# Value rows of the global tokens gathered early and copied in by small transfers, and key and query loads of 80 rows, in an attention kernel with dense layers behind it

## The chip, the cores and the metric

The kernel runs on one core of one Trainium2 chip. The metric is the device time of one execution in microseconds. An execution of the profiled kind gives in addition a trace: every instruction of the engines TensorE (PE, with its weight loads as PEld), VectorE (DVE), ScalarE (ACT), GpSimd (POOL) and SyncE (SP), with the semaphores between them and the packets of the DMA queues.

## The reference

Attention over a window of 32 tokens to either side, with eight global tokens that attend to all and are attended by all, and then a dense layer with an activation of x cos(x) and a second dense layer.

```python
B, H, S, D = 8, 8, 576, 64                     # 8 global tokens in global_idx
scores = matmul(q, k^T) / sqrt(D)
mask   = |i - j| <= 32  or  i is global  or  j is global
attn   = softmax(where(mask, scores, -1e9))
x      = (attn @ v) as (B * S, H * D) = (4608, 512)
h      = x @ w_in                              # (512, 2048)
out    = (h * cos(h)) @ w_out                  # (2048, 512), float32
```

## The kernel before

**Units.** Two heads of one batch are a pair; there are 32 pairs. Two pairs, so four heads, are a half batch. The first five half batches (pairs 0 to 9) are the front; they are computed while weights and most inputs are still on their way, and they take another route than the rest. The front cuts the 576 tokens of a head into five blocks of 120 keys (`NK5`), to each of which the eight global keys are added as the first eight rows (`G`). So the value tile of a half batch, `vw`, has 128 partitions: eight rows of global values, 120 rows of local ones.

**The order** of all work is written by hand. The string `FRONT` lists the steps of the front, one word each; `MID`, `FIFTH`, `SIXTH` and `ORDER` list the later half batches. A step issues its instructions on each engine's queue at the place where it stands, and each engine runs its own queue in order. The letters that matter here, with the number of the pair or half batch behind them:

- `L`: `load_qk`, two DMAs from GpSimd's queue that bring key and query of a half batch into `kn` and `qn`, as fp16, eight tokens in one row of 1 KB per head, so 72 rows for 576 tokens (three buffers; the third, `kn[2]` and `qn[2]`, lies in the space of `w_out16`).
- `M`: `next_values`, which clears 64 rows of the first block of a value buffer on VectorE, and then `load_vn`, five DMAs from SP that bring the half batch's values into `vn32` as fp32. `vn32` has room for four half batches, and half batch 4 takes the place of half batch 2.
- `C`: `cast_vn`, one GpSimd instruction that turns these into fp16 in `vw`. Ahead of it, from half batch 2 on, stands a copy of one element that waits for the newest mask product.
- `y`: `value_rows`, for the two heads of a pair: five matmuls with `one_v`, a matrix of zeros and ones that picks the global tokens out of the blocks, add up to the eight rows of global values in a bank of PSUM (tag `h`), and a copy on ScalarE writes them to the first eight rows of all five blocks of `vw`. Since `one_v` multiplies every row, the first eight rows of `vn32` have to hold numbers; `clear_rows` sets them to zero.
- `k`, `q`: transposes of key and query on TensorE into a bank of tag `h`, and copies on ScalarE to `kw` and `qb`. For pairs 4 to 9 the global columns are put in by GpSimd (`g`), from `kgT` and `qgT`, which step `H1` turns on TensorE and copies on VectorE.
- `s`: scores of a pair, ten matmuls into four banks, then four exponentials on ScalarE (`e`) and three products with the mask on VectorE (`pm`).
- `f`: matmuls of ones, whose result nobody reads, into a spare part of `pv`.
- `p`: values of a pair, 20 matmuls into the one buffer `pv`, then sums, reciprocals and the product `xn` on VectorE.
- `x`: transposes of `xn` on TensorE, copies into `xT` on VectorE.
- `E`, `Y`, `H`: gathers of the global rows of key and query, and (`Y0`) of value, for the first four batches by GpSimd, each as two indirect DMAs with the row numbers `gidx_rows`; `H2` turns the gathered values to fp16 for later half batches.
- `n`: sum of squares of `xn` on ScalarE. `W`, `O`: weight loads. `m`, `t`: the first dense matmuls and their activation.

The dense layers' instructions are `mlp_in` (`ph`), `mlp_act` (`cos`, `g`) and `mlp_out` (`po`); they start behind pair 8 and then run among the later pairs.

**Semaphores of the DMAs.** The DMAs of SP use eight semaphores in turn, and those of GpSimd eight others. A DMA whose semaphore has been used waits on its queue until the one eight before it has landed. A DMA that reads or writes what others make waits for those in addition.

Of the kernel before, what the change touches and what calls it, by code (L numbers as in the profile page):

```python
# [10 lines left out]
FP16 = mybir.dt.float16  # L11
# [6 lines left out]
B, H, S, D = 8, 8, 576, 64  # L18
# [5 lines left out]
G = 8  # L24
# [2 lines left out]
KL = 32  # L27
HY = 5
PK = 4
RW = 8  # L30
KS = 120
NK5 = 5
KPAD = 3
KP = KPAD + S // RW
QP = S // RW + 4
OFF = (0, 136, 488, 680, 328)
# [5 lines left out]
C = G + QB  # L42
# [10 lines left out]

SIXTH = "sa 2 2 2 2 sz pa 1 1 2 xa pz G 1 1 2 xz n 1 1 D0 2 kc qc D1 1 D2 2 1"

FRONT = ("M1 s0 E0 C0 E1 L2 w6 k1 q1 w4 s1 y0.0 f8 k2 q2 C1 H0 p0 M2 L3 y0.1 s2 k3 q3 f6 x0 p1 M3 H1 g4 g5 g6 C2 y1.0 s3 g7 L4 I k4 q4 f6 x1 p2 M4 y1.1 s4 "
         "C3 W0 k5 q5 f6 x2 p3 y2.0 s5 g8 g9 W1 W2 W3 k6 q6 f6 x3 p4 y2.1 s6 C4 Y0 k7 q7 f6 x4 p5 n0 y3.0 s7 k8 q8 f6 x5 p6 y3.1 s8 H2 k9 q9 f6 x6 p7 y4.0 s9 "
         "x7 p8 y4.1 O m m x8 K5 p9 t t + m m t t x9 -")
WARM = 13
OK_ALL = float(P * (B * NP * 2 * BP + B))  # L60

# [143 lines left out]
def kernel(  # L205
# [10 lines left out]
    nc = tc.nc  # L216
# [5 lines left out]
    keep = es.enter_context(tc.tile_pool(name="keep", bufs=1))  # L222
# [27 lines left out]
    NN = 3  # L250
    kT = [keep.tile([P, 2, KT], FP16, name=f"kT{i}") for i in range(2)]
    qT = [keep.tile([P, 2, QT], FP16, name=f"qT{i}") for i in range(2)]
    kn = [keep.tile([KP, 2 * 2, RW, D], FP16, name=f"kn{i}") for i in range(2)]
    qn = [keep.tile([QP, 2 * 2, RW, D], FP16, name=f"qn{i}") for i in range(2)]
    w_out16 = const.tile([P, NF, DM], FP16)
    kn.append(w_out16[0:KP, 0:4].rearrange("p h (r d) -> p h r d", d=D))
    qn.append(w_out16[0:QP, 4:8].rearrange("p h (r d) -> p h r d", d=D))
# [17 lines left out]
    def load_qk(s, hs=(0, 4)):  # L275

        base = (s * 4 + hs[0]) * S * D
        for src, dst in ((k, kn[s % NN][KPAD : KPAD + S // RW]), (q, qn[s % NN][0 : S // RW])):
            nc.gpsimd.dma_start(dst[:, hs[0] : hs[1]].rearrange("x h r d -> x h (r d)"),
                                dview(src, base, (RW * D, S // RW), (S * D, hs[1] - hs[0]), (1, RW * D)))  # L280

    def turn_half(s):

# [6 lines left out]
    vg32 = keep.tile([P, 2, 2, D], FP32)  # L290
# [16 lines left out]
    def pick_globals(pr, t, src, ones, n, to):  # L307

        h0 = 2 * (pr % 2)
        for r in range(RW):  # L310
            for h in range(2):
                nc.tensor.matmul(t[h * D : (h + 1) * D], src[:n, h0 + h, r], ones[:n, r], start=r == 0, stop=r == RW - 1, skip_group_check=True)
        nc.scalar.copy(to, view(t, (0, to.shape[1]), (1, G)))

    def warm(n, tag="s"):

        t = ps.tile([P, 4, P], FP32, tag=tag, bufs=2 + (tag == "s"))
        for _ in range(n):
# [13 lines left out]
    def gather(src, dst, half):  # L332
        rows = src.rearrange("b h s d -> (b h s) d")
        for h in range(2):
            nc.gpsimd.indirect_dma_start(
                out=dst[:, half, h], out_offset=None, in_=rows,
                in_offset=bass.IndirectOffsetOnAxis(ap=gidx_rows[:, 0:1], axis=0),
                element_offset=(half * 32 + h) * S * D)
# [23 lines left out]
    def vn_of(s):  # L362
        i = s if s < 4 else 2
        return view(vn32[i // 2][:, 4 * (i % 2)], (4 * D, NK5), (1, 4 * D))
# [13 lines left out]
        nc.vector.memset(vn_of(s)[0:64, 0], 0.0)  # L378
        load_vn(s)

    def clear_rows(s):

        nc.gpsimd.memset(vn_of(s)[0:G, 1:], 0.0)

    gate = keep.tile([1, 1], FP16)

# [513 lines left out]
    with tc.manual_schedule():  # L900
# [2 lines left out]
        nc.vector.memset(ones16, 1.0)  # L903
        nc.vector.memset(pio2, pi / 2.0)
        nc.vector.memset(kn[0][0:KPAD, 0:2], 0.0)
        for t in (qn[0][64:QP, 2:4], kn[0][0:KPAD, 2:4], qn[1][64:QP], kn[1][0:KPAD], qn[2][64:QP], kn[2][0:KPAD]):
            nc.scalar.memzero(t.rearrange("p a b c -> p (a b c)"))
        load_qk(0, (0, 2))
        nc.gpsimd.iota(p_i, pattern=[[0, 1]], base=0, channel_multiplier=1)
# [12 lines left out]
        build_band()  # L922
        index_rows(1)
        load_vn(0)
        for s in range(1, 4):
            clear_rows(s)
        load_qk(1)
        build_ones()
        build_mask5()
# [60 lines left out]
            load_values(2 * s)  # L990
            load_values(2 * s + 1)

        def late_gathers(_):

            gather(v, vg32, 0)

        LOCAL = {"k": local_k, "q": local_q}
        OTHER = LOCAL | {"g": globals_kq, "L": load_qk, "W": load_w_in, "v": load_values, "n": x_squares,
                 "C": cast_vn, "I": row_numbers, "E": early_rows, "w": lambda n: warm(n, "h" if n == 6 else "s"), "y": value_rows, "M": next_values, "N": clear_rows, "Y": late_gathers, "V": hold, "U": hold_x, "H": early_globals, "Z": steady_buffers, "f": fill, "r": load_vn, "A": later_rows, "D": later_globals, "O": load_w_out, "K": lambda s: cast_half(s, "vkq"), "B": bring, "m": lambda _: one(False), "t": lambda _: mlp_act()}
        ready[0] = 1  # L1000
        for step in FRONT.split():
            if step in "+-":
                spare[0] = step == "+"
                continue
            f = (STEPS | OTHER)[step[0]]
            f(*[int(x) for x in (step[1:] or "0").split(".")])
        ready[0], front[0] = 2, False
        for s in range(4, B * NP // 2):
            outs_by[0] = 8 * (s - 3)
            for step in {4: MID, 5: FIFTH, 6: SIXTH}.get(s, ORDER).split():  # L1010
# [20 lines left out]
                else:  # L1031
                    f, pr = (STEPS | OTHER)[step[0]], 2 * s + "azcd".index(step[1])
# [56 lines left out]
```

## Time and profile before

| | us |
|---|---|
| median of 3 runs | 351.18 |
| lowest and highest | 351.07 and 353.2 |
| the profiled execution | 349.19 |
| its span, first to last instruction | 347.3 |
| PE, DVE, ACT, POOL busy in the span | 329.4, 249.5, 246.0, 110.0 |

Times in the profile count from the start of the span. A row of the timeline has start, duration, engine, line, operation, out<-in, shape, how many, and in brackets the idle time of the engine ahead of it and what ended that. A row of the chain of waits has start, duration and what the end of the kernel hung on in that time; "issue" is time in which the profile shows no wait. A row of a stretch has its bounds, its length, the busy time of PE, PEld, DVE, ACT and POOL with the number of instructions, the granted clock of TensorE, the mean busy share of the DMA engines (over 1 where packets overlap) and GB/s.

### The profile page before, as it was taken

The numbers are of one execution on the slowest core, as the hardware profiler recorded it, in microseconds if no ns is written. First come the engines' busy times: TensorE is split into PE (matmuls) and PEld (weight loads), VectorE is DVE, ScalarE is ACT, GpSimd is POOL, SyncE is SP. The second block draws the span as 40 slices with busy tenths as digits, with TensorE's granted clock in tenths as the row PEclk, the third lists the DMA queues.
The fourth block names the chain that finished last, engine by engine and source line by source line (L and its number), as shares of the span: only waits on it lengthen the run. The fifth ranks groups of instructions, "written<-read, shape, count | busy, mean of one in ns | idle before, by whom it ended". The sixth has DMA issues, their size and how long they took to land.

```text
span 347.3 us, 8464 instructions
## 1 busy us (share of the span) xinstructions
PE 329.4 (95%) x3207; PEld 172.7 (50%) x3207; DVE 249.5 (72%) x611; ACT 246.0 (71%) x423; POOL 110.0 (32%) x221
## 2 busy tenths in 40 slices
PE   7977989999989999999999999999999999999993
PEld 3566865444445454545454545454545344444442
DVE  6665778987597688888797878788888466556310
ACT  8878797796566896878787777878787866644300
POOL 8754846632352506050705062325001000000000
PEclk9999899999999999999999999999999999999997
DMA  5998992999999999999999999999990001100112
GB/s 78 185 165 152 171 195 39 187 175 153 162 153 195 149 155 137 183 150 194 140 171 156 192 142 182 126 219 145 139 134 2 32 30 59 34 31 30 62 60 69
DMA packets 165891, 44.58 MB, mean 128 GB/s; under 512 B 153764, under 2 KB 160996, under 8 KB 165668
## 3 DMA queue, kind: packets, MB, share of 16 engines
q1 hardware_dynamic: 105860, 26.70, 51.5%
q0 software_dynamic: 59984, 17.28, 49.6%
q8 instruction: 27, 0.44, 0.5%
q14 instruction: 20, 0.16, 0.2%
HBM read 44.41 MB, written 19.17 MB: 183 GB/s over the span
## 4 chain that ended last, share of the span: by engine, by line
PE 81%; ACT 6%; DVE 4%; issue 3%; DMA 2%; SPq 1%; POOL 1%; ACTq 0%; POOLq 0%; DVEq 0%
PE po L800 34%; PE ph L762 34%; PE pv L719 3%; PE st L699 3%; PE tx L744 2%; DMA gidx_col<-in_global_idx_dram 1%; ACT e L638 1%; DMA vn<-in_v_dram 1%; PE po L782 1%; PE t L319 1%; PE pv L646 1%; ACT e L634 1%; ACT cos L768 1%; DVE g L769 1%; DVE xn L666 1%
## 5 line engine op out<-in xcount | busy, mean ns | idle before, releaser
L762 PE MATMUL ph<-xT,w_in 128*128 128x512 f16 x576 | 139.3, 379 | 1.1 <-DVE g L769 1.0
L800 PE MATMUL po<-w_out,g 128*128 128x512 f16 x560 | 136.8, 379 | 0.0
L768 ACT ACTIVATE cos<-ph,pio 128x512 f16<-128x512 f32 x144 | 97.0, 687 | 55.3 <-PE ph L762 51.6
L769 DVE TENSOR_TENSOR g<-cos,ph 128x512 f16<-128x512 f16 x144 | 96.5, 685 | 45.6 <-ACT cos L768 43.4
L800 PEld LDWEIGHTS <-g 128*128 128x128 f16 x560 | 53.6, 98 | 63.7
L762 PEld LDWEIGHTS <-w_in 128*128 128x128 f16 x576 | 53.9, 98 | 62.7 <-issue 1.4
L702 ACT ACTIVATE e<-st 128x512 f16<-128x512 f32 x44 | 23.9, 594 | 10.0 <-PE st L699 9.9
L980 POOL COPY gate<-xn 1x1 f16<-1x1 f16 x8 | 1.4, 180 | 81.9 <-DVE xn L730 81.9
L703 DVE TENSOR_TENSOR pm<-e,mask 128x512 f16<-128x512 f16 x44 | 18.7, 425 | 11.7 <-ACT e L702 10.3
L752 POOL COPY xT<-xg 128x4 f16 x48 | 15.4, 320 | 31.5 <-DVE xT L747 28.9
L272 POOL DMA_DIRECT2D q<-in_q_dram x11 | 24.0, 2183 | 0.0
L818 ACT ACTIVATE xn<-xn 128x1536 f16<-128x1536 f16 (+1 forms) x16 | 22.6, 1413 | 0.0
L730 DVE TENSOR_TENSOR xn<-pv,r_all 128x768 f16<-128x768 f32 x22 | 21.1, 957 | 1.0
L805 ACT COPY o<-po 128x512 f32<-128x512 f32 x17 | 10.0, 586 | 14.7 <-PE po L800 14.7
L807 DVE COPY o<-po 128x512 f32<-128x512 f32 x18 | 12.4, 690 | 9.0 <-PE po L800 8.5
L272 POOL DMA_DIRECT2D k<-in_k_dram x11 | 18.1, 1644 | 0.9 <-issue 0.9
L768 ACT ACT_TABLE_LOAD x12 | 15.4, 1283 | 0.2
L702 ACT ACT_TABLE_LOAD x11 | 14.1, 1283 | 0.2
L607 DVE COPY kw<-kT 128x1320 f16<-128x1320 f16 x22 | 13.9, 630 | 0.0
L699 PEld LDWEIGHTS <-kw 64*128 64x128 f16 x484 | 8.4, 95 | 10.7 <-issue 8.1
L579 POOL COPY kw<-kgT 128x88 f16<-128x88 f16 x22 | 12.8, 716 | 0.1
L699 PE MATMUL st<-qb,kw 64*128 64x64 f16 x484 | 11.2, 191 | 1.5 <-DVE qb L619 1.1
(185 smaller groups left out, 391.0 us busy)
## 6 DMA issues: line engine op xcount, KB each, us to landing
out_dram<-o SPq DMA_DIRECT2D x35, 256.0 KB
vw<-v SPq DMA_DIRECT2D x32, 165.0 KB
v<-in_v_dram POOLq DMA_DIRECT2D x11, 288.0 KB, 5.5
k<-in_k_dram POOLq DMA_DIRECT2D x11, 288.0 KB, 8.7
q<-in_q_dram POOLq DMA_DIRECT2D x11, 288.0 KB, 11.5
vn<-in_v_dram SPq DMA_DIRECT2D x20, 120.0 KB
w_in<-in_moe_w_in_dram POOLq DMA_DIRECT2D x4, 512.0 KB, 10.0
w_out<-in_moe_w_out_dram POOLq DMA_DIRECT2D x1, 2048.0 KB, 15.3
```

The costliest lines, as they stand in the source:

```text
L272: nc.gpsimd.dma_start(dst[s].rearrange("t (h d) -> t h d", h=4), dview(src, base, (D, S), (S * D, 4), (1, D)))
L607: nc.vector.tensor_copy(to, view(kT[pr // 2 % 2][:, pr % 2], (QB, NB), (1, W)))
L699: nc.tensor.matmul(st[j // 8 * 2 + h][:, j % 8 * C : j % 8 * C + C], kp[hp, j], qp[hp, j], start=True, stop=True)
L702: nc.scalar.activation(e[:, 0:512], st[h], AF.Exp, scale=scale)
L703: nc.vector.tensor_tensor(view(pm[:, h], (1, 512)), e[:, 0:512], view(mask, (1, 512)), ALU.mult)
L730: nc.vector.tensor_tensor(view(xn, (384, 2), (D, 6), (1, D)), view(pv, (512, 2), (65, 6), (1, D)), view(rp, (6, 2), (1, 6), (0, D)), ALU.mult)
L752: nc.gpsimd.tensor_copy(xT[:, :, bass.ds(pool_idx[g] + b * S, 1)], xg[:, :, g : g + 1])
L762: nc.tensor.matmul(ph, w_in16[:, j, f * P : (f + 1) * P], xT[:, j, t * TT : (t + 1) * TT], start=(j == 0), stop=(j == NC - 1))
L768: nc.scalar.activation(cos, ph, AF.Sin, bias=pio2)
L769: nc.vector.tensor_tensor(g, cos, ph, ALU.mult)
L800: nc.tensor.matmul(po, g16[:, f, s * P : (s + 1) * P], w_out16[:, f], start=(f == 0), stop=(f == NF - 1))
L818: nc.scalar.activation(view(xn, (BP * P, 2), (1, n)), view(xn, (BP * P, 2), (1, n)), AF.Square, accum_out=x_sq[:, s : s + 1])
```

## The change

Four edits go together.

1. The gather of global value rows of the first four batches (two indirect DMAs of GpSimd) moves from the middle of the front (`Y0`, which goes) to its head, into the place of the three `clear_rows`, which go too.
2. For half batches 1 to 4 (pairs 2 to 9), `value_rows` goes. In its place a new step `S`, `spread_vg`, copies the eight gathered rows of a pair from `vg32` into the first eight rows of all five blocks of `vn32`, by one DMA on SP behind the half batch's loads, ahead of the cast. Half batch 0 keeps `value_rows`.
3. `load_qk` of half batches 1 to 4 brings 80 rows: for the keys three rows ahead of the half batch's own and five behind, for the queries eight behind. The rows that used to be zero now hold tokens of neighbours, which the mask leaves out; so the zeroing of those rows on ScalarE goes for the buffers 1 and 2. Half batch 0 keeps 72 rows.
4. In `FRONT` the scores of pair 3 move from behind the turning of globals (`H1`), the casts of half batch 2 and `y1.0` to a place ahead of them, and all fills but those of `f8` go from six matmuls to four.

```diff
+KQ = 80
-FRONT = ("M1 s0 E0 C0 E1 L2 w6 k1 q1 w4 s1 y0.0 f8 k2 q2 C1 H0 p0 M2 L3 y0.1 s2 k3 q3 f6 x0 p1 M3 H1 g4 g5 g6 C2 y1.0 s3 g7 L4 I k4 q4 f6 x1 p2 M4 y1.1 s4 "
-         "C3 W0 k5 q5 f6 x2 p3 y2.0 s5 g8 g9 W1 W2 W3 k6 q6 f6 x3 p4 y2.1 s6 C4 Y0 k7 q7 f6 x4 p5 n0 y3.0 s7 k8 q8 f6 x5 p6 y3.1 s8 H2 k9 q9 f6 x6 p7 y4.0 s9 "
-         "x7 p8 y4.1 O m m x8 K5 p9 t t + m m t t x9 -")
+FRONT = ("M1 S2 S3 s0 E0 C0 E1 L2 w6 k1 q1 w4 s1 y0.0 f8 k2 q2 C1 H0 p0 M2 S4 S5 L3 y0.1 s2 k3 q3 f4 x0 p1 M3 S6 S7 s3 H1 g4 g5 g6 C2 g7 L4 I k4 q4 f4 x1 p2 M4 S8 S9 s4 "
+         "C3 W0 k5 q5 f4 x2 p3 s5 g8 g9 W1 W2 W3 k6 q6 f4 x3 p4 s6 C4 k7 q7 f4 x4 p5 n0 s7 k8 q8 f4 x5 p6 s8 H2 k9 q9 f4 x6 p7 s9 "
+         "x7 p8 O m m x8 K5 p9 t t + m m t t x9 -")
 def load_qk(s, hs=(0, 4)):
-        for src, dst in ((k, kn[s % NN][KPAD : KPAD + S // RW]), (q, qn[s % NN][0 : S // RW])):
-            nc.gpsimd.dma_start(dst[:, hs[0] : hs[1]].rearrange("x h r d -> x h (r d)"),
-                                dview(src, base, (RW * D, S // RW), (S * D, hs[1] - hs[0]), (1, RW * D)))
+        for src, dst, n, lead in ((k, kn[s % NN], KQ, KPAD), (q, qn[s % NN], KQ, 0)):
+            if s == 0:
+                dst, n, lead = dst[lead:], S // RW, 0
+            nc.gpsimd.dma_start(dst[0:n, hs[0] : hs[1]].rearrange("x h r d -> x h (r d)"),
+                                dview(src, base - lead * RW * D, (RW * D, n), (S * D, hs[1] - hs[0]), (1, RW * D)))
-    def clear_rows(s):
-        nc.gpsimd.memset(vn_of(s)[0:G, 1:], 0.0)
+    def spread_vg(pr):
+        nc.sync.dma_start(vn_of(pr // 2)[0:G, :, 2 * D * (pr % 2) : 2 * D * (pr % 2 + 1)],
+                          view(vg32[pr * G : (pr + 1) * G, 0], (0, NK5), (1, 2 * D)))
-        for t in (qn[0][64:QP, 2:4], kn[0][0:KPAD, 2:4], qn[1][64:QP], kn[1][0:KPAD], qn[2][64:QP], kn[2][0:KPAD]):
+        for t in (qn[0][64:QP, 2:4], kn[0][0:KPAD, 2:4]):
             nc.scalar.memzero(t.rearrange("p a b c -> p (a b c)"))
         load_vn(0)
-        for s in range(1, 4):
-            clear_rows(s)
+        gather(v, vg32, 0)
         load_qk(1)
-        def late_gathers(_):
-            gather(v, vg32, 0)
```

The tiles `kn` and `qn` are given 80 rows instead of 75 and 76.

More of the change, by code (lines that the diff above doesn't have):

```diff
@@ L252 @@
     qT = [keep.tile([P, 2, QT], FP16, name=f"qT{i}") for i in range(2)]
-    kn = [keep.tile([KP, 2 * 2, RW, D], FP16, name=f"kn{i}") for i in range(2)]
-    qn = [keep.tile([QP, 2 * 2, RW, D], FP16, name=f"qn{i}") for i in range(2)]
+    kn = [keep.tile([KQ, 2 * 2, RW, D], FP16, name=f"kn{i}") for i in range(2)]
+    qn = [keep.tile([KQ, 2 * 2, RW, D], FP16, name=f"qn{i}") for i in range(2)]
     w_out16 = const.tile([P, NF, DM], FP16)
-    kn.append(w_out16[0:KP, 0:4].rearrange("p h (r d) -> p h r d", d=D))
-    qn.append(w_out16[0:QP, 4:8].rearrange("p h (r d) -> p h r d", d=D))
+    kn.append(w_out16[0:KQ, 0:4].rearrange("p h (r d) -> p h r d", d=D))
+    qn.append(w_out16[0:KQ, 4:8].rearrange("p h (r d) -> p h r d", d=D))
     vw = [keep.tile([P, NB, 2, D + 1], FP16, name=f"vw{i}") for i in range(NV)]
@@ L991, in bring @@
             load_values(2 * s + 1)
-        def late_gathers(_):
-            gather(v, vg32, 0)
         LOCAL = {"k": local_k, "q": local_q}
         OTHER = LOCAL | {"g": globals_kq, "L": load_qk, "W": load_w_in, "v": load_values, "n": x_squares,
-                 "C": cast_vn, "I": row_numbers, "E": early_rows, "w": lambda n: warm(n, "h" if n == 6 else "s"), "y": value_rows, "M": next_values, "N": clear_rows, "Y": late_gathers, "V": hold, "U": hold_x, "H": early_globals, "Z": steady_buffers, "f": fill, "r": load_vn, "A": later_rows, "D": later_globals, "O": load_w_out, "K": lambda s: cast_half(s, "vkq"), "B": bring, "m": lambda _: one(False), "t": lambda _: mlp_act()}
+                 "C": cast_vn, "I": row_numbers, "E": early_rows, "w": lambda n: warm(n, "h" if n == 6 else "s"), "y": value_rows, "M": next_values, "S": spread_vg, "V": hold, "U": hold_x, "H": early_globals, "Z": steady_buffers, "f": fill, "r": load_vn, "A": later_rows, "D": later_globals, "O": load_w_out, "K": lambda s: cast_half(s, "vkq"), "B": bring, "m": lambda _: one(False), "t": lambda _: mlp_act()}
         ready[0] = 1
```

## The prediction

> **What bounds the kernel now.** I read the page first, then busy time by stretch, then the chain of waits inside the front, and last the waits and the timeline around each instruction that the change removes.
>
> ```profile
> span 347.3 us, 8464 instructions
> PE 329.4 (95%) x3207; PEld 172.7 (50%) x3207; DVE 249.5 (72%) x611; ACT 246.0 (71%) x423; POOL 110.0 (32%) x221
> 30.00:40.00 10.00, 7.55 (x134) 6.29 (x128) 5.89 (x22) 6.58 (x15) 7.15 (x14) 0.83 0.80 138
> 40.00:50.00 10.00, 8.69 (x213) 7.53 (x209) 7.44 (x24) 10.00 (x24) 7.23 (x16) 1.00 1.21 189
> 60.00:70.00 10.00, 10.00 (x48) 4.53 (x47) 9.47 (x26) 7.92 (x13) 6.06 (x6) 1.00 1.19 188
> 200.00:250.00 50.00, 50.00 (x494) 25.28 (x492) 41.54 (x94) 39.21 (x63) 17.53 (x38) 1.00 1.46 162
> ```
>
> In a stretch's row the columns are length, PE, PEld, DVE, ACT, POOL, the granted clock, the DMA share and GB/s. From 60 us on PE is full: the dense layers end the kernel, and nothing here touches them. So the change is worth what it takes off the front, which ends when the first dense matmuls start. From 40 to 50 us ACT has no free time; from 30 to 40 us no engine is full, and the chain says why (the last row is from the waits: who waited for whom, us in total, times, longest):
>
> ```profile
> 20.60 0.28 DVE vn L378
> 22.84 3.53 DMA vn<-in_v_dram
> 26.87 4.57 issue
> 31.56 1.26 POOL vw L402
> 32.93 0.27 DVE vn L378
> DVE vn L378 <- POOL vw L402: 2.9, 1, 2.9
> ```
>
> The value loads of half batch 2 start after the clearing at 20.60. GpSimd, ready at 26.9, waits until they have landed, casts at 31.56 (step C2), and only then may VectorE clear the same buffer for half batch 4 (M4, at 32.93). That clearing stands in VectorE's order ahead of the mask products of pair 4, so 2.9 us of VectorE are lost. I call it the gate. Behind it:
>
> ```profile
> 36.13 0.81 PE L493 MATMUL pv<-ones 128*128 128x184 f16 x6 [0.26 <-DVE xn L666]
> 37.27 1.59 PE L646 MATMUL pv<-vw,pm 128*128 128x65 f16 x20
> 38.86 0.55 PE rows L409 x5
> 39.32 0.79 PE L631 MATMUL st<-qb,kw 64*128 64x136 f16 x10
> 39.43 0.69 ACT L410 CAST vw<-rows 8x640 f16<-8x640 f32 x1 [2.14 <-PE rows L409]
> 40.02 1.01 ACT L634 ACTIVATE e<-st 128x488 f16<-128x488 f32 x2
> 44.00 0.19 ACT xn L818
> 44.19 0.58 ACT vw L410
> 47.50 0.69 ACT L410 CAST vw<-rows 8x640 f16<-8x640 f32 x1
> 47.72 0.55 PE L631 MATMUL st<-qb,kw 64*128 64x136 f16 x10 [0.26 <-ACT qb L616]
> 48.13 1.04 ACT L634 ACTIVATE e<-st 128x488 f16<-128x488 f32 x2
> ```
>
> ACT is idle for 2.14 us before the row copy of pair 6 (39.43); then it runs the exponentials of pairs 6, 7, 8, 9 in turn, and the front ends with pair 9.
>
> **The change part by part.** *Row matmuls and copies (steps y1.0 to y4.1), pair 6.* Eight groups of five matmuls and eight copies go; only those behind the gate count, because what is saved ahead of it waits at the gate. Pair 6: PE loses the row matmuls (0.55 in the chain) and two fills of six (0.81 x 2/6 = 0.27), so its scores start at 39.32 - 0.82 = 38.50. The first six of ten scores take 0.79 x 6/10 = 0.47, so the exponential can start near 39.0 instead of 40.02, with no copy ahead: 1.0 us gained.
>
> *Pair 7.* Its copy stands between the sum of squares (ends 44.19) and the exponential, with nothing to hide it: 0.58.
>
> ```order
> L818 ACTIVATE xn,x_sq<-xn 128x2x640
> L410 COPY vw_95<-rows 8x5x2x64
> L634 ACTIVATE e<-st 128x488 x2
> L638 ACTIVATE e<-st 128x384 x2
> ```
>
> This is ScalarE before, at pair 7 (xn squares, then the copy of value rows, then the exponential e). Ahead of it now, with line numbers four higher:
>
> ```order
> L822 ACTIVATE xn,x_sq<-xn 128x2x640
> L638 ACTIVATE e<-st 128x488 x2
> L642 ACTIVATE e<-st 128x384 x2
> ```
>
> The copy is gone and the exponential follows the squares.
>
> *Pairs 8 and 9.* The copy at 47.50 covers a wait that stays: the scores start at 47.72 when ACT has made qb, six of ten take 0.33, so the exponential could not start before 48.05, and it starts at 48.13. Gain 0 to 0.1; I take 0. Pair 9 has the same order. Sum behind the gate: 1.6 us.
>
> *The gate itself.* In place of the row matmuls SP now copies gathered rows into the value buffer, and C2 waits for that too.
>
> ```order
> L373 DMA vn_118<-in_v_dram 96x4x64 [waits DMAHW5_49,DVE_49]
> L373 DMA vn_118<-in_v_dram 120x4x64 [waits DMAHW6_49]
> L373 DMA vn_118<-in_v_dram 120x4x64 [waits DMAHW7_49]
> L373 DMA vn_118<-in_v_dram 120x4x64 [waits DMAHW0_49]
> L373 DMA vn_118<-in_v_dram 120x4x64 [waits DMAHW1_49]
> L373 DMA vn_118<-in_v_dram 96x4x64 [waits DMAHW2_49,DVE_49]
> ```
>
> So SP stood before at half batch 2 (vn is the value buffer; the last row belongs to half batch 3). Now:
>
> ```order
> L376 DMA vn_118<-in_v_dram 120x4x64 [waits DMAHW3_49]
> L386 DMA vn_118<-vg_106 8x5x128 [waits DMAHW4_49]
> L386 DMA vn_118<-vg_106 8x5x128 [waits DMAHW5_49]
> L376 DMA vn_118<-in_v_dram 96x4x64 [waits DMAHW6_49,DVE_49]
> ```
>
> Two transfers of 8 x 5 x 128 floats, 20 KB each, stand between the last load of half batch 2 and the first of half batch 3. Their price is bounded by these rows:
>
> ```profile
> 24.50:29.00 4.50, 3.28 (x79) 2.82 (x80) 3.15 (x13) 3.71 (x9) 1.33 (x7) 1.00 1.10 182
> 40.75:41.25 0.50, 0.50 (x11) 0.50 (x8) 0.50 (x2) 0.50 (x2) 0.50 (x2) 1.00 0.95 143
> 42.00:43.00 1.00, 0.82 (x17) 0.68 (x18) 1.00 (x6) 1.00 (x4) 0.88 (x4) 1.00 1.22 187
> L414 SPq DMA_DIRECT2D vw<-vg x44: 685/714/2304, 80.6 to 254.5; - x44
> L373 SPq DMA_DIRECT2D vn<-in_v_dram x25: 317/482/2478, 2.5 to 35.2; - x25
> kn<-in_k_dram POOLq DMA_DIRECT2D x3, 288.0 KB, 6.4
> ```
>
> Below, 41 KB at 182 GB/s: 0.22 us. Above, two issues like those of the other 8-row copies (714 ns median): 1.43 us. I take 0.3, near the lower end: the queue is backed up (the last load, issued at 22.84, lands only at 31.4), so issuing is covered. Were SP not early, 1.43 would show; it is, since its next load waited for the clearing of half batch 3 at 25.04 anyway.
>
> Against this stand the loads with 80 rows. Around 41 us only a 72-row query load moves: 143 GB/s. Once 128-row weight loads move beside it: 187. At these rates a 72-row load of 288 KB takes 2.06 us, one of 80 rows (320 KB) 1.75: 0.31 less. Two of them share the queue with the loads of half batch 2 (key and query of half batch 3), so 0.6 earlier. If the 80 rows kept the slower rate, they would cost 2.29 - 2.06 = 0.23 each, 0.46 in all; if the two loads ahead count too, the gain is 1.24. I take 0.6, since row counts and rates differ just as stated. Gate: 0.3 - 0.6 = -0.3 us.
>
> [...]
>
> *Head.* The early gather takes GpSimd's place where three clearings stood, and a gather leaves the queue at 45.78:
>
> ```profile
> 5.62 2.75 POOL L383 MEMSET vn<- 8x1024 f32 x3
> 45.78 1.04 POOL L335 DMA_INDIRECT vg<-in_v_dram,gidx_rows  x1 [0.16 <-issue]
> 47.12 1.00 POOL L335 DMA_INDIRECT vg<-in_v_dram,gidx_rows  x1 [0.30 <-issue]
> 16.33 0.47 PE L595 MATMUL bank<-ident,kn 75*64 75x75 f16 x16
> 20.06 1.25 POOL L402 CAST vw<-vn 128x1280 f16<-128x1280 f32 x1 [1.50 <-DMA vn<-in_v_dram]
> ```
>
> 1.04 + 0.30 + 1.00 + 0.3 against 2.75: the key and query loads behind it are issued as before, and pair 2 reads them at 16.33. SP's first two copies wait for the gather; behind them on SP is nothing that can start before 20.60. They may push the cast of half batch 1 from 20.06 to 20.4, with the loads of half batch 3 behind it on GpSimd; pair 2's values, its reader, run at 27.3. Cost 0. The four zeroings gone from ACT end before its first copy, which needs a query load anyway: 0.
>
> *Order.* The scores of pair 3 move ahead of the turning of globals, and fills fall from six to four; both lie ahead of the gate or are counted.
>
> Sum: 1.0 + 0.58 + 0.3 = 1.9 us. The profiled execution took 349.19 (span 347.3) and would take 347.3; it is 2.0 below the median of the runs, 351.18. So **349.3 us**.
>
> **The rivals.** *Late rows (slower than before).* Place: the two copies between half batches 2 and 3 on SP. If each issue takes the longest seen among value loads, 2.478 us, and C2 waits for it, the gate moves by 4.96 - 0.6 = +4.4, and the time is 351.18 - 1.6 + 4.4 = 354.0. It decides from a shift of 1.6 on. For: the queue is saturated then (DMA share 1.10). Against: the median of such copies is 0.71.
>
> *Hidden anyway.* VectorE or the value accumulators set the pace behind the gate and only the gate's 0.3 remains: 350.9. For: VectorE is busy 7.44 of 10 us at 40 to 50. Against: ACT has 10.00 there.
>
> *Clock.*
>
> ```profile
> 36.75:39.00 2.25, 2.25 (x31) 2.09 (x29) 1.18 (x6) 0.53 (x1) 1.73 (x3) 0.50 0.99 157
> 34.85 0.34 PE L631 MATMUL st<-qb,kw 64*128 64x192 f16 x4 [1.23 <-DVE xg L684]
> 35.43 0.44 PE L595 MATMUL bank<-ident,qn 76*64 76x76 f16 x16
> ```
>
> After the idle PE at the gate the granted clock is 0.50 near 38 us. With less filling it may fall one window earlier; the work from 34.85 to 35.87, 1.0 us, would take 2.0, some 0.7 of it late for the fills that now start at 36.13: 350.0. If it did not fall at all, the fills and values behind 36.13 would gain about as much: 348.6. [...]
>
> *No gate.* If the faster loads let C2 run before VectorE asks for it, the 2.9 us wait goes too: 351.18 - 1.6 - 2.9 = 346.7. For: copies gone ahead of the gate let pairs run ahead to it. Against: landing would have to come 3 us earlier, and 1.24 is the most that I can derive.
>
> That the rows are not what they were, or the matmuls stay, is excluded by the order shown.
>
> **How the numbers follow.** The forecast has 0.46, late rows 0.13, hidden 0.18, clock 0.14, no gate 0.09. Low end: 351.18 - 1.6 - 1.24 - 0.7 = 347.6. High end: 351.18 - 1.6 + 1.43 + 0.7 = 351.7. Left out are no gate and most of late rows, under 0.2. What this kernel's runs can tell from no change is about 1%, 3.5 us: faster by more is no gate with some of the forecast's low tail, 0.10; slower by more takes late rows at a shift beyond 5, just past the price above, 0.06; the rest, 0.84, is within.
>
> **What would show it.** In the changed profile: C2's cast near 31.3 and the clearing near 32.6; the exponential of pair 6 near 38.8 instead of 40.02, that of pair 7 near 42.8 instead of 44.67, and pairs 8 and 9 1.9 earlier; a 72 against 80 row rate of 143 against about 187 GB/s; the first dense matmuls 1.9 us earlier and the dense part as long as now. A cast later than 33.2, or a pair spacing that grows by what the copies gave back, would make the prediction wrong.

## The result, and the profile after

| | before | after |
|---|---|---|
| median, lowest and highest of 20 runs each (us) | 351.38 (349.18 to 354.16) | 350.42 (346.62 to 353.49) |
| the profiled execution, its span (us) | 349.19, 347.3 | 350.42, 348.7 |

The ratio of after to before is 0.9944 (95% interval 0.992 to 0.9968), so the change gains about 2 us in these runs, as forecast. A second set of runs (after, again, below) has 0.9981 (0.9942 to 1.002), a gain of about 0.7 us, and doesn't exclude that there is none. The two profiles of the table don't show a gain: after's execution is the longer one by 1.2 us. Before's was among the fastest (of its 20 runs only 349.18 is lower), after's lies on its median. So what follows reads places, and not differences of spans. Ratios leave out the runs that took over 1.5% more than the fastest of their kernel, and where a profile came from such a run (the six fills and the version with everything, below), only its front is read.

The stretches of after, in the order of those of before (length, PE, PEld, DVE, ACT, POOL, clock, DMA share, GB/s):

```profile
span 348.7 us, 8349 instructions
30.00:40.00 10.00, 6.45 (x111) 5.29 (x109) 5.95 (x21) 4.63 (x12) 7.03 (x15) 0.72 0.98 165
40.00:50.00 10.00, 9.35 (x194) 8.04 (x189) 8.32 (x25) 9.09 (x22) 5.58 (x15) 0.77 1.24 206
60.00:70.00 10.00, 10.00 (x48) 4.52 (x47) 9.39 (x26) 8.24 (x12) 5.03 (x5) 1.00 1.22 196
200.00:250.00 50.00, 50.00 (x494) 25.32 (x492) 41.52 (x94) 39.25 (x64) 18.67 (x40) 1.00 1.46 161
```

ACT got the time of its copies back (from 40 to 50 us: 10.00 before, 9.09 now). But the clock, 0.83 and 1.00 before, is 0.72 and 0.77. The front's timeline in after, first the value buffers (the rows from SP's queue are DMA issues, L376 the loads, L386 the small copies; POOL L282 are the key and query loads), then the exponentials of pairs 6 to 9:

```profile
22.51 1.44 POOL L406 CAST vw<-vn 128x1280 f16<-128x1280 f32 x1 [3.85 <-DMA vn<-vg]
24.37 0.64 POOL L282 DMA_DIRECT2D kn<-in_k_dram  x1
24.42 1.88 SPq L386 DMA_DIRECT2D vn<-vg  x2
31.51 1.25 POOL L406 CAST vw<-vn 128x1280 f16<-128x1280 f32 x1 [3.73 <-DMA vn<-in_v_dram]
32.88 0.27 DVE L381 MEMSET vn<- 64x256 f32 x1 [3.91 <-POOL vw L406]
39.32 1.04 ACT L638 ACTIVATE e<-st 128x488 f16<-128x488 f32 x2 [2.77 <-PE st L635]
43.96 1.04 ACT L638 ACTIVATE e<-st 128x488 f16<-128x488 f32 x2 [0.40 <-PE st L635]
47.46 1.04 ACT L638 ACTIVATE e<-st 128x488 f16<-128x488 f32 x2 [0.51 <-PE st L635]
50.96 1.05 ACT L638 ACTIVATE e<-st 128x488 f16<-128x488 f32 x2 [0.50 <-PE st L635]
```

The gate stands where it stood: cast at 31.51 (31.56 before), clearing at 32.88 (32.93). Two things changed ahead of it and cancel. The cast of half batch 1 waits for a small copy, which lands at 22.4, and comes at 22.51 instead of 20.06; the key and query loads of half batch 3, behind it on GpSimd, leave at 24.37 instead of 22.09. With these out of the way, the value loads of half batch 2 land by 28.6 us (31.4 before). These landings are from the semaphore records of the trace, the last record of each DMA. But the two small copies, issued at 24.42 and 25.61, land only at 30.6 and 31.3. The row of the cast puts the wait down to the value loads; by the semaphores it was the copies. Behind the gate pair 6 is 0.70 us earlier than before, and pair 9 0.71.

PE's waits of 0.5 us and more between 60 and 150 us, before first, then after:

```profile
PE st L699 <- DVE qb L619: 1.1, 1, 1.1
```

```profile
PE st L703 <- DVE qb L623: 1.8, 1, 1.8
PE pv L723 <- DMA vw<-vg: 1.5, 2, 1.2
```

So the dense part got longer: PE arrives earlier (the first dense matmuls start at 53.00 us, 53.94 before) and waits 0.7 us more for a query and 1.5 us for later half batches' global value rows, of which before had nothing that it waited for.

### The profile page after: what moved, and what is told of

It reads as the page before. It is cut to its first block, busy times and chain, and to the rows that moved or that the text cites. A ratio compares the mean times of both kernels' runs of the same rounds, so it can differ in the third digit from the quotient of the medians.

```text
span 348.7 us, 8349 instructions
## 1 busy us (share of the span) xinstructions
PE 328.8 (94%) x3153; PEld 172.3 (49%) x3153; DVE 249.4 (72%) x611; ACT 237.3 (68%) x411; POOL 106.4 (31%) x218
## 4 chain that ended last, share of the span: by engine, by line
PE 75%; DVE 7%; DMA 6%; ACT 5%; SPq 3%; issue 3%; POOL 1%; ACTq 0%; DVEq 0%
PE po L804 30%; PE ph L766 29%; DMA q<-in_q_dram 3%; PE pv L723 3%; PE t L322 2%; PE st L703 2%; DVE g L773 2%; PE tx L748 2%; DMA vw<-vg 2%; PE pv L650 2%; ACT cos L772 1%; DMA vn<-in_v_dram 1%; PE po L786 1%; DVE xn L670 1%; SPq L418 1%
## 5 line engine op out<-in xcount | busy, mean ns | idle before, releaser
L707 DVE TENSOR_TENSOR pm<-e,mask 128x512 f16<-128x512 f16 x44 | 18.7, 425 | 11.0 <-ACT e L706 9.6
L756 POOL COPY xT<-xg 128x4 f16 x48 | 15.9, 330 | 32.3 <-DVE xT L751 29.6
L638 ACT ACTIVATE e<-st 128x488 f16<-128x488 f32 x20 | 10.4, 572 | 9.0 <-PE st L635 6.4
L723 PE MATMUL pv<-vw,pm 128*64 128x65 f16 x484 | 12.8, 197 | 1.5 <-DMA vw<-vg 1.5
```

What stands on the lines that cost most here:

```text
L707: nc.vector.tensor_tensor(view(pm[:, h], (1, 512)), e[:, 0:512], view(mask, (1, 512)), ALU.mult)
L723: nc.tensor.matmul(pv[r0 : r0 + C, j // 6, c0 : c0 + 65], pm[:, h, j], vp[:, j, h], start=True, stop=True)
L756: nc.gpsimd.tensor_copy(xT[:, :, bass.ds(pool_idx[g] + b * S, 1)], xg[:, :, g : g + 1])
```

## The experiments

The kernels of the experiments were timed in 12 runs each, beside 17 to 35 of before on the same chip; after's own ratio is that of the result. Each kernel has one profile, and after has two. The table has what decides in the front of each profiled execution: when the key load of half batch 3 leaves GpSimd's queue, the cast of half batch 2, how long VectorE's clearing for half batch 4 waited for it, the exponentials of pairs 6 and 9, and the microseconds at a halved clock between 15 and 60 us.

| kernel | key load | cast | wait | pair 6 | pair 9 | halved | ratio to before |
|---|---|---|---|---|---|---|---|
| before | 22.09 | 31.56 | 2.9 | 40.02 | 51.67 | 3.4 | 1 |
| after | 24.37 | 31.51 | 3.9 | 39.32 | 50.96 | 10.2 | 0.9944 (0.992 to 0.9968) |
| after, again | 25.80 | 28.39 | - | 37.08 | 48.21 | 6.8 | 0.9981 (0.9942 to 1.002) |
| rows first | 26.27 | 29.38 | - | 38.09 | 49.24 | 10.2 | 0.9995 (0.9957 to 1.0033) |
| 72 rows | 24.28 | 31.52 | 3.8 | 39.33 | 50.66 | 3.4 | 0.9975 (0.9939 to 1.001) |
| six fills | 27.08 | 32.66 | - | 42.19 | 53.32 | 10.2 | 0.9915 (0.9869 to 0.9962) |
| before, 80 rows | 22.73 | 31.68 | 2.9 | 40.11 | 52.75 | 3.4 | 1.0035 (0.9998 to 1.0071) |
| rows twice | 26.66 | 33.95 | 4.2 | 41.76 | 53.40 | 10.2 | 1.0029 (0.9989 to 1.007) |
| rows early | 26.25 | 29.27 | - | 37.52 | 48.65 | 6.8 | 0.9918 (0.9882 to 0.9955) |
| no rows | 21.95 | 32.53 | 5.0 | 40.68 | 51.81 | 6.8 | 0.9973 (0.9933 to 1.0012) |
| copies back | 25.89 | 29.55 | - | 38.43 | 50.08 | 6.8 | 0.9896 (0.9853 to 0.9938) |
| load held | 26.87 | 29.18 | - | 39.50 | 50.63 | 6.8 | 1.0017 (0.9986 to 1.0048) |
| all | 24.48 | 33.64 | 6.3 | 41.45 | 53.09 | 13.7 | 0.9995 (0.9962 to 1.0027) |
| held and filled | 26.40 | 28.89 | 1.1 | 36.76 | 47.90 | 3.4 | 0.9934 (0.9899 to 0.997) |

**Rows first.** The small copies of half batches 2 to 4 go ahead of the five value loads.

```diff
         nc.vector.memset(vn_of(s)[0:64, 0], 0.0)
+        if s > 1:
+            spread_vg(2 * s)
+            spread_vg(2 * s + 1)
         load_vn(s)
```

> The changed kernel, with the two small row copies of half batches 2, 3 and 4 issued on SP ahead of the five value loads instead of behind them; same work. In the changed kernel's profile the loads of half batch 2 have landed at 28.6 us, the second row copy lands at 31.3 and the cast runs at 31.51. Theory A, the small copies are now what the gate waits for: with the copies ahead the cast follows the last load, at 29 to 30, the clearing of half batch 4 comes at 30.3 to 31.4 instead of 32.88, and the time falls by 1 to 2 us against the changed kernel (ratio to the kernel before 0.989 to 0.992). Theory B, the queue as a whole is what drains at 31.4, whatever stands last in it: cast at 31.2 to 31.7, ratio 0.994 as now.

Cast at 29.38, no gate, pair 9 1.7 us earlier than in after; the time didn't follow (ratio 0.9995). One window of 3.4 us was halved behind the front as well, from 52.7 us on, which takes 1.7 us back (half of it, an estimate: from 52.7 to 56.1 us PE is busy for 3.40 of 3.40 us, at a clock of 0.50).

**72 rows.** The changed kernel with the old key and query loads, and ScalarE's four zeroings back.

```diff
-            if s == 0:
+            if s < 9:
                 dst, n, lead = dst[lead:], S // RW, 0
```

> The changed kernel with loads of 72 rows for key and query, and the zeroing on ScalarE back; gather and small copies stay. If the 80 rows are worth what the prediction gave them, 0.6 us at the gate, the cast of half batch 2 moves from 31.5 to about 32.1 and the time is 0.6 us above that of the changed kernel (ratio to before 0.996). If the row count does nothing there, the cast stays within 0.2 us of 31.5 and the ratio at 0.994.

The cast comes at 31.52 and the exponential of pair 6 at 39.33, both within 0.01 us of after: at the gate the 80 rows give nothing. Pair 7 is at 43.41 (43.96 in after), with 3.4 us of halved clock instead of 10.2.

**Six fills.** The changed kernel with every `f4` as `f6` again.

> The changed kernel with six filling matmuls a pair again instead of four. In the profiled run of the changed kernel the clock was halved for 10.24 us from 34.37, before for 3.41 us from 36.45. If fewer fills cause the longer dip, it shrinks to 3.4 or 6.8 us, the mean granted clock rises above 0.985 and the time falls by 0.5 to 1 us (ratio 0.991 to 0.993). If the dip comes from TensorE waiting at the gate, which fills do not cover, it stays, and the fills add about 0.2 us a pair where TensorE is on the chain: ratio 0.994 to 0.997.

The ratio is the second best of all, with an interval that overlaps after's. Its profile shows a front that a stop of PE of 3.33 us held up (last section), so the profile tells nothing on the fills. The ratio is where the expectation put it if fewer fills lengthen the halved clock, but the interval doesn't exclude that the fills do nothing: what the fourth edit's cut of the fills costs stays open.

**Before, 80 rows.** The other way round: before with the 80-row loads alone.

> The kernel before, with the 80-row loads alone. By the prediction the cast of half batch 2 moves from 31.56 to about 31.0 and the time falls by 0.6 us (ratio 0.998). If the row count does nothing at the gate: cast at 31.4 to 31.7, ratio 1.000. If the larger loads cost their extra bytes, cast at 32.0, ratio 1.001.

Cast at 31.68 and pair 6 at 40.11, 0.1 us later than in before; the time shows no gain, and rather a loss. So the 80 rows are worth nothing here, with the other edits or without them.

**Rows twice.** The suspected copies, doubled.

```diff
-... p0 M2 S4 S5 L3 y0.1 ...
+... p0 M2 S4 S5 S4 S5 L3 y0.1 ...
```

> Issues the two small copies of half batch 2 twice, one pair after the other, with the same contents. Late rows (the copies, issued behind the value loads, hold the cast of half batch 2): the cast moves from 31.51 us to between 33 and 36, the exponential of pair 6 from 39.3 to 41 or later, and the kernel loses 1.5 to 4 us against the changed kernel. Loads set the cast: it stays within 0.3 us of 31.5 and the time within 0.5 us. Clock: the cast moves, the time goes by the number of halved clock windows and may stand still.

The cast moves to 33.95 and pair 6 to 41.76, both 2.4 us later than in after, and the ratio goes from 0.9944 to 1.0029. So copies behind the value loads can set the cast: the late rows of the prediction's first rival. The second pair of copies leaves SP at 29.13 and 29.92, when the first pair has landed, behind key and query loads that left at 26.66; it lands at 33.2 and 33.8, and the cast follows. PE's hole of 2.13 us at 21.9 us (last section) delayed this front too, so not all of the 2.4 us is theirs.

**Rows early.** The buffers of half batches 2 and 3 are cleared at the start, and their small copies follow those of half batch 1.

```diff
-M1 S2 S3 s0 ... M2 S4 S5 L3 ... M3 S6 S7 s3 ...
+M1 S2 S3 S4 S5 S6 S7 s0 ... M2 L3 ... M3 s3 ...
```

> The buffers of half batches 2 and 3 are cleared at the start, and their four small copies follow those of half batch 1 on SP, at about 18 to 21 us, ahead of all value loads of half batch 2. Late rows: the cast of half batch 2 comes with its loads, at 28.5 to 29.5 us instead of 31.5, the clearing for half batch 4 at 30 to 32, the exponential of pair 6 at 37 to 38.3, pair 9 1 to 2 us earlier, and the time falls by 1 to 2 us against the changed kernel. Loads set the cast: it stays at 31.5. Clock: the front ends earlier but a halved window falls behind it, and the time stays within 0.5 us of the changed kernel.

As expected of late rows: cast at 29.27, pair 9 2.3 us earlier than in after, ratio 0.9918. But the key load had moved too (26.25), so this run alone doesn't say which of the two did it.

**No rows.** The one that speaks against the copies as the whole cause. This kernel leaves out the global values of half batches 1 to 4, so it stands for the timing of the front alone; the clearings and the late gather (`Y0`) return.

```diff
-M1 S2 S3 s0 ... M2 S4 S5 L3 ... M3 S6 S7 s3 ... M4 S8 S9 s4 ... C4 k7
+M1 s0 ... M2 L3 ... M3 s3 ... M4 s4 ... C4 Y0 k7
...
-        gather(v, vg32, 0)
+        for s in range(1, 4):
+            clear_rows(s)
```

> The changed kernel without the global value rows of half batches 1 to 4 (no early gather, no small copies; the three clearings on GpSimd and the late gather are back): what the removal of matmuls and copies gives by itself. Late rows: the cast of half batch 1 is back near 20.1 us (22.5 in the changed kernel), the cast of half batch 2 comes at 28.5 to 29.5, and the kernel is 1 to 2.5 us faster than the changed one. Rows cost nothing (the gate is set by the loads): cast at 31.5, time as the changed kernel within 0.5 us.

Neither theory had it. Without any small copy the value loads land at 32.3 us and the cast comes at 32.53, later than with the copies, and VectorE waits 5.0 us. What is different: the cast of half batch 1 waits for no copy, and the key load leaves at 21.95. The timeline of this kernel, the two casts, the load and the clearing:

```profile
19.86 1.25 POOL L410 CAST vw<-vn 128x1280 f16<-128x1280 f32 x1 [1.00 <-DVE r_all L669]
21.95 0.64 POOL L282 DMA_DIRECT2D kn<-in_k_dram  x1
32.53 1.25 POOL L410 CAST vw<-vn 128x1280 f16<-128x1280 f32 x1 [4.83 <-issue]
33.90 0.27 DVE L381 MEMSET vn<- 64x256 f32 x1 [5.02 <-POOL vw L410]
```

That gave the third theory, collision: the key and query loads of half batch 3 (640 KB) and the value transfers of half batch 2 move at the same time (in after, from 24.4 to 31.3 us, packets of GpSimd's queue take 62.1% and those of SP's 55.4% of the DMA engines' time); if the former leave early, the latter land late and the gate closes.

**Copies back.** The row matmuls and ScalarE's copies of half batches 3 and 4 return beside the gathered rows.

```diff
-p5 n0 s7 k8 ... p6 s8 H2 ... p7 s9 ... p8 O
+p5 n0 y3.0 s7 k8 ... p6 y3.1 s8 H2 ... p7 y4.0 s9 ... p8 y4.1 O
```

> The changed kernel with the four groups of row matmuls and ScalarE's four row copies of half batches 3 and 4 put back behind the gate, beside the gathered rows. The sum of the prediction: pair 6 and pair 7 pay together what was counted as gained, less the fills, so the exponential of pair 7 comes 1.0 to 1.4 us later than in the changed kernel, pairs 8 and 9 as much, and the time rises by 1.0 to 1.4 us. Hidden anyway: the exponentials of pairs 8 and 9 stay within 0.3 us, and the time stays.

Up to the gate the instructions are those of after, yet the front took another course: key load at 25.89, cast at 29.55, no wait. (PE's hole of 1.85 us at 21.3 us, last section, is in this front too.) The ratio, 0.9896, is the best of all. A loss of 1.0 to 1.4 us, as expected, would have made 0.997 to 0.998, outside its interval; so the copies that the change removes aren't what the kernel's time hung on, as far as kernels that can take two courses (below) can be compared by ratios. Behind the gate the rows show what the copies cost, against the second profile of after (first the copies back, then after again; pairs 5 to 9):

```profile
34.87 1.05 ACT L638 ACTIVATE e<-st 128x488 f16<-128x488 f32 x2 [0.50 <-PE st L635]
38.43 1.05 ACT L638 ACTIVATE e<-st 128x488 f16<-128x488 f32 x2 [0.52 <-PE st L635]
43.09 1.01 ACT L638 ACTIVATE e<-st 128x488 f16<-128x488 f32 x2
46.53 1.04 ACT L638 ACTIVATE e<-st 128x488 f16<-128x488 f32 x2
50.08 1.01 ACT L638 ACTIVATE e<-st 128x488 f16<-128x488 f32 x2
```

```profile
33.51 1.05 ACT L638 ACTIVATE e<-st 128x488 f16<-128x488 f32 x2 [0.50 <-PE st L635]
37.08 1.05 ACT L638 ACTIVATE e<-st 128x488 f16<-128x488 f32 x2 [0.52 <-PE st L635]
41.16 1.09 ACT L638 ACTIVATE e<-st 128x488 f16<-128x488 f32 x2
44.71 1.05 ACT L638 ACTIVATE e<-st 128x488 f16<-128x488 f32 x2 [0.50 <-PE st L635]
48.21 1.04 ACT L638 ACTIVATE e<-st 128x488 f16<-128x488 f32 x2 [0.50 <-PE st L635]
```

From pair to pair: 3.56, 4.66, 3.44, 3.55 with copies and 3.57, 4.08, 3.55, 3.50 without. The copy costs 0.58 us at pair 7 and, over pairs 8 and 9, nothing. On pair 6 this kernel tells nothing, though the expectation counts it: the copy ahead of that pair's exponential, at 39.43 in before, belongs to `y2.1` of half batch 2, which is not put back. The step at pair 7 is the same elsewhere: from pair 6 to pair 7 it takes 4.65 or 4.66 us in the three profiles with the copy, and 4.07 to 4.09 in the eight without it whose clock is full again ahead of pair 7's scores.

**Load held.** Only the start of the key and query loads is moved: they wait for the mask products of pair 3.

```diff
+    def load_held(s):
+        nc.gpsimd.tensor_copy(gate, pm_of[max(pm_of)][0:1, 2 * CN - 1 : 2 * CN])
+        load_qk(s)
...
-M2 S4 S5 L3 y0.1 ... M3 S6 S7 s3 H1 ...
+M2 S4 S5 y0.1 ... M3 S6 S7 s3 T3 H1 ...
```

> The changed kernel with one thing moved: the key and query loads of half batch 3 wait on GpSimd for the mask products of pair 3 (near 26.4 us) instead of following the cast of half batch 1 (24.4 us there, 21.95 us in the kernel without rows). Collision (these loads and the value loads of half batch 2 share the DMA engines, whichever starts late loses, and the gate opens where the value loads win): the cast of half batch 2 at 29 to 29.8 us, VectorE's clearing no longer waited for, the exponential of pair 6 at 37.5 to 38.8, that of pair 9 between 48.5 and 50.3 instead of 50.96, time 1 to 2 us below the changed kernel. Late rows (the small copies, issued at 24.4 and 25.6, set the cast): it stays at 31 to 31.5 and the time stays.

Its timeline, with the small copies of half batch 2, the key load, the cast and the exponential of pair 6:

```profile
24.59 1.44 SPq L391 DMA_DIRECT2D vn<-vg  x2
26.87 0.65 POOL L282 DMA_DIRECT2D kn<-in_k_dram  x1 [0.33 <-PE bank L604]
29.18 1.25 POOL L411 CAST vw<-vn 128x1280 f16<-128x1280 f32 x1
39.50 1.04 ACT L643 ACTIVATE e<-st 128x488 f16<-128x488 f32 x2 [2.28 <-PE st L640]
```

And from its waits between 34 and 41 us, who waited for whom:

```profile
PEld L604 <- DMA qn<-in_q_dram: 2.1, 1, 2.1
```

The small copies leave at the time they left in after (24.59; 24.42 there), the loads 2.5 us later, and the copies land at 27.8 us instead of 31.3 (semaphore records): the cast comes at 29.18. This is what collision said. But GpSimd was free for the loads at 25.65 here, so the hold moved them by 1.2 us only, and after opens its gate at times without a hold (next); this profile alone doesn't settle it. The time stays: now pair 6 waits 2.1 us for its own query load, which lands at 35.9 us, and pairs 6 and 9 (39.50, 50.63) are later than collision had them.

**After, again.** The same program a second time.

> The changed kernel once more, for a second profile and more times. If its front has one course: cast of half batch 2 within 0.3 us of 31.5, exponential of pair 9 within 0.5 us of 50.96 apart from what the clock does. If small shifts of the DMA traffic pick between two courses, as the kernel with the copies back suggests (its instructions up to the gate are the same ones, and its cast came at 29.55), the cast comes either near 31.5 or near 29.5, and the times fall in two groups about 2 us apart.

The timeline of this second profile: the two casts and the key load between them, the exponential of pair 4, and the clearing:

```profile
23.77 1.25 POOL L406 CAST vw<-vn 128x1280 f16<-128x1280 f32 x1 [5.40 <-DVE r_all L666]
25.80 0.65 POOL L282 DMA_DIRECT2D kn<-in_k_dram  x1
28.39 1.25 POOL L406 CAST vw<-vn 128x1280 f16<-128x1280 f32 x1 [0.22 <-DMA vn<-vg]
30.01 1.05 ACT L638 ACTIVATE e<-st 128x488 f16<-128x488 f32 x2 [2.14 <-PE st L635]
30.85 0.27 DVE L381 MEMSET vn<- 64x256 f32 x1
```

And two of its stretches, cut where the clock changed:

```profile
47.20:50.60 3.40, 1.70 (x33) 1.24 (x33) 3.33 (x12) 2.88 (x6) 0.14 (x1) 1.00 1.24 206
50.60:54.00 3.40, 3.40 (x17) 1.29 (x14) 1.82 (x8) 1.41 (x2) 2.18 (x9) 0.50 0.51 86
```

One program, two courses. The small copy that the cast of half batch 1 waits for landed at 23.6 us instead of 22.4, the cast came 1.3 us later than in the first profile, so the key load left at 25.80 and the gate was open: pair 9 at 48.21 instead of 50.96. The price is a wait at pair 4 (2.14 us: what PE needs to turn the globals is cast on GpSimd behind that cast), and later a halved window from 50.6 us on, which takes 1.7 us back (half of the 3.40 us that PE is busy there, an estimate). The times, 347.77 to 352.64 us, don't split cleanly into two groups, and the ratio, 0.9981, is a smaller gain than that of the first set.

**All.** Rows early, the casts of key and query globals ahead of the cast of half batch 1 (`H0 C1` for `C1 H0`), and six fills behind the scores of pair 9 (`s9 f6`).

> The kernel with the early small copies, and two things more: GpSimd casts the key and query globals ahead of the cast of half batch 1 (there PE waited 1.64 us for them, and pair 4 started 2.1 us late), and six fills stand behind the scores of pair 9, where PE was half idle and the clock was halved in the window after (51.1 to 54.5 us). If the wait is what delays pair 4: its exponential moves from 30.45 to between 28 and 29.3, pair 9 from 48.65 to between 46.5 and 47.8. If idle PE there brings the halved window: it goes, worth 1.7 us. Together 1.5 to 3.5 us below the kernel with early copies alone, about 345 to 347.5 us. If L3 and the value loads collide anew, the cast of half batch 2 goes back to 31 or later and the time stays at 348 to 350.

From its timeline the key load, the exponential of pair 4, the cast and the clearing:

```profile
24.48 0.65 POOL L282 DMA_DIRECT2D kn<-in_k_dram  x1
27.70 1.05 ACT L639 ACTIVATE e<-st 128x488 f16<-128x488 f32 x2 [0.87 <-PE st L636]
33.64 1.25 POOL L407 CAST vw<-vn 128x1280 f16<-128x1280 f32 x1 [6.07 <-DMA vn<-in_v_dram]
35.01 0.27 DVE L382 MEMSET vn<- 64x256 f32 x1 [6.25 <-POOL vw L407]
```

The wait at pair 4 went as expected (27.70), but with the two casts no longer between the cast of half batch 1 and the loads, these left at 24.48: cast at 33.64, the collision that the expectation named last. The time fell back to that of before.

**Held and filled.** After with `H0 C1`, `s9 f6`, and the loads held for the first mask products of pair 3.

> The changed kernel with three things: GpSimd casts the key and query globals ahead of the cast of half batch 1 (so that pair 4 needn't wait for them), the key and query loads of half batch 3 wait for the first mask products of pair 3 (so that they leave between 25.6 and 26.2 us however late that cast is, the time at which the good course of the changed kernel had them, 25.80), and six fills stand behind the scores of pair 9. Collision theory: cast of half batch 2 at 28.3 to 29.3 us, exponential of pair 4 at 27.5 to 28.2, of pair 9 at 46.7 to 48.7, no halved window between 47 and 54 us, span 344 to 346 and time 345.5 to 348, that is ratio 0.982 to 0.99. If the start of these loads isn't what decides, or pair 4 coming earlier collides anew: cast at 31 or later, pair 9 at 50.5 or later, time 350 or more. If these loads come too late for pair 6: its exponential at 39 or later with a wait for its scores, pair 9 near 50, time 349 to 351.

Key load at 26.40, cast at 28.89, pair 9 at 47.90, the earliest of all; no halved window behind pair 9. Pair 4 was at 28.50 and pair 6 waited 1.76 us for its scores. The ratio, 0.9934, falls short of the expected 0.982 to 0.99: of 3.8 us of front some 2.3 us of time were left. PE now waits 1.5 us from 60 to 150 us for the copies of later half batches' global rows, as in after.

No version is faster than after by more than the intervals leave open; the best, copies back, six fills and rows early, are 0.9896, 0.9915 and 0.9918.

## Why the prediction was right or wrong

**The time** was forecast at 349.3 us with 347.6 to 351.7 as its range, and is 350.42; the gain was put at 1.9 us and the ratio says 2.0 (0.7 in the second set of runs). The sum behind it does not hold, so that the number came so near is luck: pair 9 should have come 1.9 us earlier, and came 0.71 us earlier in one profile and 3.46 in the other.

**Pair 7, 0.58**: right, as the copies put back show (4.66 against 4.08 us from pair 6 to pair 7). In the first profile of after it doesn't appear (43.96 - 39.32 = 4.64, before 4.65) since PE's scores, at a halved clock until 44.6 us, come 0.40 us after ACT is free. In the kernel with 72 rows, whose clock is full from 39.4 us on, the same step is 4.08. **Pairs 8 and 9, 0**: right.

**Pair 6, 1.0**: mis-sized, 0.65 beside the gate's 0.05. Its scores started at 38.70, where the sum with the gate had 38.20, and its exponential came 0.62 us behind them, where the sum had 0.47. PE's clock was 0.50 from 34.4 us on (before: from 36.45). A stretch of after's first profile shows it; then the end of the fills and pair 6's scores, first what follows the fills in before, then the fills, what follows them and the scores in after:

```profile
34.40:37.80 3.40, 2.96 (x53) 2.88 (x51) 3.05 (x11) 2.15 (x6) 1.94 (x6) 0.50 0.94 143
```

```profile
36.73 0.74 PE L678 MATMUL tx<-ident,xn 128*128 128x128 f16 x5
```

```profile
36.08 0.77 PE L497 MATMUL pv<-ones 128*128 128x184 f16 x4 [0.45 <-DVE xn L670]
36.64 0.74 PE L682 MATMUL tx<-ident,xn 128*128 128x128 f16 x5
38.70 0.91 PE L635 MATMUL st<-qb,kw 64*128 64x136 f16 x10
```

Six fills held PE from 36.13 to 36.73 before, until 36.45 at full clock; four held it from 36.08 to 36.64 now, all the time at half. So two fills less gave 0.04 us and not 0.27. This is the clock rival's place. The rival was priced at one window (3.41 us in before, from 36.45 us on), and the halved clock lasted three (10.24 us, from 34.37 us on), but the windows ahead of 36 us cost pair 6 nothing: with 72 rows the clock was halved from 35.96 us only, and its exponential came at 39.33 all the same. That the clock falls earlier with less filling was the rival's estimate and is not shown: with four fills in both, it was halved for 10.2 us in after and for 3.4 with 72 rows. No run puts the copy ahead of pair 6 back, so this term is read from places and not tested.

**The gate, -0.3**: the step that failed, by three of its parts. *Two 80-row loads, -0.6*: nothing, from both sides (31.68 against 31.56, 31.52 against 31.51). The term has 80 rows move at the 187 GB/s of 128-row loads, which no run shows. In a stretch in which key and query loads move in both, the rates do differ: first the 72 rows, then after, with 80.

```profile
37.00:38.50 1.50, 1.50 (x23) 1.34 (x21) 0.78 (x4) 0.00 (x0) 1.19 (x2) 0.50 1.08 169
```

```profile
37.00:38.50 1.50, 1.50 (x23) 1.34 (x22) 0.77 (x4) 0.00 (x0) 1.25 (x2) 0.50 1.21 197
```

That is a factor of 1.17 (197 against 169 GB/s for all transfers together), and not the 1.31 of the prediction's 187 and 143; whatever it is, the gate doesn't hang on it. *Small copies, +0.3*: they landed 2.7 us after the value loads that they follow (31.3 against 28.6), so the place of "late rows" was right and 0.3 too small, though the cast didn't get later than before. *Cast of half batch 1 "from 20.06 to 20.4 ... Cost 0"*: it came at 22.51 and 23.77. The prediction named the key and query loads behind it and costed only the reader of the cast, pair 2's values. Their start is what decides: where they leave by 24.5 us the cast of half batch 2 comes at 31.5 or later, in all six profiles; where they leave from 25.8 to 26.9 us it comes at 28.4 to 29.6, in all six that have neither doubled copies nor the longest hole in PE. By the semaphore records the last transfer that the cast needs lands at 31.3 to 33.5 us in the first six and at 27.8 to 29.3 in the others, six fills included (29.2; there GpSimd itself was late). Edits that let these loads leave earlier (no rows; all, against rows early) made that transfer land later (no rows: 32.3 us, against 31.3 in after), and edits that held them (load held; held and filled) made it land earlier (load held: 27.8).

So where the gate opens, the change works mostly by a side effect: its new wait holds GpSimd, GpSimd holds a transfer, and the transfer stays out of the way of one that is needed sooner. "No gate", excluded since a landing 3 us earlier could not be derived from the faster rows, came true in the second profile by this way.

**The dense part as long as now**: wrong. 2.2 us of new waits in the first profile, a halved window and 0.7 us of waits in the second.

**Open**: in what share of executions after takes which course, and what lets the small copy that the cast of half batch 1 waits for land at 22.4 or 23.6 us in executions of one program. That the time of after hangs on the courses is argued from two profiles, not shown run by run. What the fills cost is open too.

## What to carry to other kernels

Cost a new wait by everything that is queued behind it, transfers above all, and ask for each what it will then collide with, or get out of the way of: a delay can be the gain. Where several DMA streams overlap, take a second profile of the same program before reading any place of the first as fixed. And look for the window in which PE is half idle before shortening a stage: three of the earlier fronts here (rows first, rows early, after again) gave part of their gain back to it (PE busy for 1.13 of 3.40, 1.75 of 3.50 and 1.70 of 3.40 us, and the 3.4 us behind it at a clock of 0.50 or 0.51).

## What the runs showed of the hardware

**The clock.** Between 15 and 60 us the halved stretches come in multiples of 3.41 us (3.41 in before, 10.24 in after; 3.4, 6.8, 10.2 or 13.7 in the table). Cut into windows of this length, the 14 profiles have 154 of them at full clock between 15 and 60 us (PE busy time as the union of its rows). All 17 with PE busy under 57% are followed by a halved one (in before 56% from 33.04 us on, in after 18% from 30.95), none of the 134 with more than 63%, and one of three between. The window at 47.20 us in after again (1.70 of 3.40) shows the one; the same place in the copies back, 66% busy, the other (its stretches):

```profile
48.40:51.80 3.40, 2.25 (x41) 1.62 (x40) 3.28 (x11) 3.40 (x8) 0.15 (x1) 1.00 1.24 204
51.80:55.20 3.40, 3.40 (x44) 2.18 (x42) 2.59 (x9) 2.40 (x4) 1.64 (x9) 1.00 0.67 113
```

Out of the halved state none of the nine windows with less than 95% led (in after 87% from 34.37 us on); 18 of 21 above did (in before 100% from 36.45). So matmuls that look hidden, like those of the value rows, may pay for themselves; this is argued from these two profiles, and not tested further.

**Stops of PE.** In three profiles PE stops inside one group of small matmuls, always behind the eleventh of sixteen, waiting for nothing that is shown: 3.33 us (six fills), 2.13 us (rows twice) and 1.85 us (copies back); in the others at most 0.7 us. This is the longest, from the timeline of the six fills:

```profile
25.16 0.28 PE L315 MATMUL bank<-one_q,qn 76*64 76x8 f16 x5 [3.33 <-issue]
```

In the packet records, a 16 KB packet of the queue that the profile calls "instruction" starts at 22.6, 21.7 and 20.9 us in these three, and between 17.9 and 19.3 us in the eleven others (18.7 in before, 18.8 in after). PE goes on 1.3 to 1.6 us after the end of that packet in all three. That PE waits for it is not shown, and what makes it late was not tried.
